# An attention and expert kernel on one core: where the sums of the input weights are made, and who adds the last key block

## The chip, the core and the metric

The kernel runs on one core of a Trainium2 chip. A core has four engines that compute, each with its own queue of instructions: TensorE (PE in the profile, PEld for its weight loads), VectorE (DVE), ScalarE (ACT) and GpSimd (POOL). SyncE (SP) only issues DMA transfers. The metric is the device time of one execution in microseconds (us); lower is better. The kernel before was run five times: median 883.84 us, from 883.41 to 883.97.

## The reference, cut to what matters

```python
# attention: 4 batches x 8 heads, 768 tokens, head size 64; 6 hash bits
q_bucket, k_bucket = hashes of q and k by the signs of q @ proj, k @ proj
mask = q_bucket[:, :, :, None] == k_bucket[:, :, None, :]
scores = np.where(mask, q @ k.T / np.sqrt(64), -1e9)
attn = np.exp(scores - scores.max(-1))
attn = attn / (attn.sum(-1) + 1e-09)
attn_out = attn @ v
# then x: 3072 tokens x 512, from all heads
h = x @ w_in            # 512 x 2048
r = np.maximum(h, 0.0)
out = (r * r) @ w_out   # 2048 x 512
```

The weights arrive as 64-bit floats; the kernel turns them into 32-bit ones itself.

## The kernel before

There are two stages. The first computes the attention, the second the two large products; this change touches only the first.

**The attention stage.** The loop `for pr in range(NP)` goes over sixteen pairs of heads. For each pair and each of six key blocks of 128 keys, `score` multiplies keys and queries on TensorE into PSUM (tiles `st`), and ScalarE takes the exponential into a tile `e`, a weight for each key and query. `attend` multiplies the values with these weights into `xo`. The softmax needs the sum over all keys as well: `add_up(pr, kt)` lets VectorE add block `kt` onto the tile `total` (128 partitions by 1536 numbers; key block 1 adds blocks 0 and 1). What is left, the sum over the 128 partitions, is made on TensorE in `sum_up` by a product with `ones` (four matmuls, one for each head and half of the queries, each to its own 32 columns of the array). VectorE turns the result over (`flip`), takes the reciprocal (`once`) and places it (`both`); TensorE spreads it over the partitions of each head (`spread`), and VectorE multiplies it into the output (`recs`, `x_t`, in `normalize`). A DMA on SP writes `x_t` to DRAM.

**Two ways to add block 5.** The dictionary `sums` names three pairs, 4, 5 and 8. In all other pairs VectorE adds blocks 1 to 5. In the three it adds only up to block 4, and `sum_up` gives TensorE a second source: the tile `e` of block 5 is multiplied with `ones` as well, four matmuls more, added up in the same PSUM tile.

**The weights beside it.** While the pairs run, the 32 pieces of both weight matrices are brought in and rounded, two pieces a pair: `load_weight` (a DMA on SP), `part_weight` on VectorE, `place_power` on ScalarE, `round_weight` on VectorE (L171, L176, L179). Pieces 0 to 15 are those of `w_in`; they stay in SBUF in two tiles, `ins[0]` (complete early in pair 4) and `ins[1]` (complete early in pair 8). The second stage multiplies by a scheme with seven products in place of eight, and for it needs sums and differences of the quarters of `w_in`. `sums_in(c)` makes four of them, `s1` to `s4`, for one of four groups of columns `c`: four VectorE instructions (L513 to L516) and, through `put_factor`, two DMAs on SP for each, which write the sum into `w_in_7` in DRAM. Before the change `sums_in(0)`, `(1)` and `(2)` stand at the end of pairs 4, 5 and 8, in the place of the add of block 5, and `sums_in(3)` at the start of pair 15.

**The order.** Each engine works through its instructions in the order in which the program issues them; this order is written out by hand. At the start of a pair VectorE has the transposes of q and k for the next pair (`features`), then `round_weight`, then `flip`, `once` and `both` for the pair before, then the add of blocks 0 and 1, then `recs` and `x_t`. TensorE has the scores of blocks 0 and 1, the hash of the next pair, `tot`, the last two `attend` of the pair before, and the spread. SP has the loads of q and k two pairs ahead, the write of a rounded piece, the load of a raw piece, then the write of `x_t`, the load of the values, and in the middle of the pair another piece. PSUM tiles of `st`, `hash` and `tot` share three buffers; `xo` has one.

The second stage loads its units of `w_in_7` from pair 13 on (`load_unit`); `load_x` and `sum_x` prepare its other operand.

Of the kernel before, what the change touches and what calls it, by code (L numbers as in the profile page):

```python
# [8 lines left out]
FP32 = mybir.dt.float32  # L9
# [6 lines left out]
ALU = mybir.AluOpType  # L16
# [18 lines left out]
def kernel(  # L35
# [10 lines left out]
    nc = tc.nc  # L46
# [6 lines left out]
    P = 128  # L53
    SB = S // P
    HS = S // 2
    NFT = DM // P
    NFF = DFF // P
    NP = B * H // 2
# [36 lines left out]
    p_t = first.enter_context(tc.tile_pool(name="p_t", bufs=1))  # L95
# [8 lines left out]
    def turn(name):  # L104

        return ps_s.tile([P, 2, 512], FP32, name=name, tag="turn")
# [4 lines left out]
    NIN = 2 * NFT  # L111
# [6 lines left out]
    def goal(i):  # L118
        if i < 2 * NIN:
            return ins[i // NIN][:, i % NIN // 2, i % 2]  # L120
        return p_t.tile([P, DM], FP32, name="out_piece", bufs=3)

    def load_weight(i):
        src, r, c = pieces[i]
        if src.dtype != U64:
            goals[i] = goal(i)
            nc.sync.dma_start(out=goals[i], in_=src[r:r + P, c:c + PIECE])
            return
        raw = p_w.tile([P, PIECE, 2], U32, name="raw", bufs=3)
        nc.sync.dma_start(  # L130
            out=raw.rearrange("p f w -> p (f w)"),
            in_=src.bitcast(U32)[r:r + P, 2 * c:2 * (c + PIECE)],
        )
        raws[i] = raw
# [64 lines left out]
    def put_factor(n, c, t):  # L199

        for f in range(NFT // 2):
            rs = t[:, f].rearrange("p (r c) -> p r c", c=P)
            nc.sync.dma_start(
                out=w_in_7[c // P:c // P + rs.shape[1], :, PLACE[n], f].rearrange("r p c -> p r c"), in_=rs
            )
# [16 lines left out]
    ones = const.tile([P, 32], FP32, name="ones")  # L222
# [156 lines left out]
    def weigh(pr):  # L379

        t = bits[pr, 1]
        nc.scalar.activation(out=t, in_=t, func=ACTF.Copy, scale=gains)

    weights = {}

    def score(pr, kt):

        e = ring[len(weights) % NRING]
        weights[pr, kt] = e
        key = slice(kt * P, (kt + 1) * P)  # L390
        sts = []

        def products(st, lo, hi, src, first):
            for h in range(2):
                rows = slice(h * D, (h + 1) * D)
                nc.tensor.matmul(  # L396
                    out=st[:, h, 0:hi - lo], lhsT=src[pr, 1][rows, key],
                    rhs=src[pr, 0][rows, lo:hi], start=first, stop=not first,
                )


        if (pr, kt) == (0, 0):
            for lo, hi in CUTS:
                sts.append(turn("st"))
                products(sts[-1], lo, hi, feat, True)
        for i, (lo, hi) in enumerate(CUTS):
            if len(sts) <= i:
                sts.append(turn("st"))
                products(sts[i], lo, hi, bits, True)
                products(sts[i], lo, hi, feat, False)  # L410
            else:
                products(sts[i], lo, hi, bits, False)
            nc.scalar.activation(  # L413
                out=e[:, :, lo:hi], in_=sts[i][:, :, 0:hi - lo], func=ACTF.Exp, scale=scale
            )

    totals, outs, recs = {}, {}, {}

    def add_up(pr, kt):

        if kt == 1:
            totals[pr] = p_n.tile([P, 2, S], FP32, name="total")
            nc.vector.scalar_tensor_tensor(
                out=totals[pr], in0=weights[pr, 0][:, :, 0:S], scalar=SB * TINY,
                in1=weights[pr, 1][:, :, 0:S], op0=ALU.add, op1=ALU.add,
            )
        else:
            nc.vector.tensor_tensor(  # L428
                out=totals[pr], in0=totals[pr], in1=weights[pr, kt][:, :, 0:S], op=ALU.add
            )  # L430
# [17 lines left out]
    def sum_up(pr, tot):  # L448


        tot = tot[:, 0]
        srcs = [totals[pr]] + [weights[pr, SB - 1]] * (pr in sums)
        for src in srcs:
            for c in range(2):
                for h in range(2):
                    g = 2 * h + c
                    nc.tensor.matmul(  # L457
                        out=tot[g * 32:(g + 1) * 32, 0:HS], lhsT=ones,
                        rhs=src[:, h, c * HS:(c + 1) * HS],
                        start=src is srcs[0], stop=src is srcs[-1],  # L460
                    )
        flip = p_n.tile([P, HS], FP32, name="flip")
        nc.vector.transpose(out=flip, in_=tot[:, 0:HS])
        once = p_n.tile([P, NB], FP32, name="once")
        nc.vector.reciprocal(
            out=once, in_=flip.rearrange("p (n f) -> p n f", f=32)[:, :, 0]
        )
        both = p_n.tile([P, 2, NB], FP32, name="both")
        nc.vector.tensor_tensor(
            out=both, in0=which,  # L470
            in1=once.rearrange("p (o n) -> p o n", o=1).to_broadcast([P, 2, NB]), op=ALU.mult,
        )
        onces[pr] = both
# [38 lines left out]
    def sums_a(a11, a12, a21, a22, s1, s2, s3, s4):  # L512
        nc.vector.tensor_tensor(out=s1, in0=a21, in1=a22, op=ALU.add)  # L513
        nc.vector.tensor_tensor(out=s3, in0=a11, in1=a21, op=ALU.subtract)
        nc.vector.tensor_tensor(out=s2, in0=s1, in1=a11, op=ALU.subtract)
        nc.vector.tensor_tensor(out=s4, in0=a12, in1=s2, op=ALU.subtract)  # L516

    def minus(out, in0, in1):
        nc.vector.tensor_tensor(out=out, in0=in0, in1=in1, op=ALU.subtract)  # L519

    NS = PIECE // 2

    def sums_in(c):

        j, h = divmod(c, 2)
        t, at = ins[j], slice(h * NS, (h + 1) * NS)
        nf = NFT // 2
        sums = [p_t.tile([P, nf, NS], FP32, name=f"s_in{n}", bufs=2) for n in range(4)]
        sums_a(
            t[:, 0:nf, 0, at], t[:, nf:NFT, 0, at], t[:, 0:nf, 1, at], t[:, nf:NFT, 1, at], *sums  # L530
        )
        for n in range(4):
            put_factor(3 + n, c * NS, sums[n])

    X_0 = 3 * PB
    sums = {NIN // 2: 0, NIN // 2 + 1: 1, NIN: 2}

    xs = {}

# [41 lines left out]
    with tc.manual_schedule():  # L584
# [21 lines left out]
        for pr in range(NP):  # L606
            a, b = 2 * pr, 2 * pr + 1
            more = pr + 1 < NP

            def prepare():  # L610

                hash_bits(pr + 1, turn("hash"))
                for w in (1, 0):
                    signs(pr + 1, w)


            if pr + 2 < NP:
                load_pair(pr + 2)
            if pr == X_0:
                load_x(0)  # L620
            if not more:
                sums_in(3)
            if more and pr > 0:
                for w in range(2):
                    features(pr + 1, w)
            if pr > 0:
                round_weight(b - 2)
                load_weight(b)
            score(pr, 0)
            if pr == 0:  # L630
                first_keys(1, turn("hash"))
            score(pr, 1)
            if pr > 0:
                finish(pr - 1, prepare if more else None)
            add_up(pr, 1)
            if pr == 0:
                for w in range(2):
                    features(1, w)
            if pr > 0:
                normalize(pr - 1)  # L640


            if pr == X_0 + 1:
                for n in range(2):
                    load_unit(n)
            part_weight(a)
            score(pr, 2)
            score(pr, 3)
            if pr == 0:
                prepare()  # L650
            elif more:
                weigh(pr + 1)
            place_power(a)
            attend(pr, 0)
            attend(pr, 1)
            for kt in (2, 3):
                add_up(pr, kt)
            if more:
                load_values(pr + 1)


            round_weight(a)
            part_weight(b)
            if more:
                load_weight(a + 2)
            score(pr, 4)
            score(pr, 5)
            if pr == 0:
                weigh(1)
            place_power(b)  # L670
            attend(pr, 2)
            attend(pr, 3)
            add_up(pr, 4)

            if pr not in sums:
                add_up(pr, 5)
            if pr in sums:
                sums_in(sums[pr])
        sum_x(0, 1)
        finish(NP - 1)  # L680
        normalize(NP - 1)
# [526 lines left out]
        for i in range(NCHUNK):  # L1208
            for s in range(NR):
# [8 lines left out]
                if i == 0 and r in THEN:  # L1218
                    m = THEN.index(r)
# [15 lines left out]
                for n in range(2):  # L1235
                    m = 2 * ((i - 1) * NR + s) + n
# [243 lines left out]
```

## Time and profile before

| | |
|---|---|
| median of five runs | 883.84 us |
| the profiled execution | 884.08 us |
| its span, from the first to the last instruction | 882.2 us |
| PE busy in the span | 867.8 us (98%) |
| PEld busy | 520.2 us (59%) |
| DVE busy | 755.7 us (86%) |
| ACT busy | 391.7 us (44%) |
| POOL busy | 106.9 us (12%) |
| granted TensorE clock | 0.997 of full speed |
| `total` adds on VectorE (L428) | 61 of 1756 ns |
| `tot` matmul records from `total` (L457) | 128, median 498 ns |
| `tot` matmul records from `e` (L457) | 24, median 486 ns |
| sums of the input weights (L513 to L516) | 16, of 682 to 692 ns |

A matmul of 32-bit floats appears as two records. Records of one engine overlap where an instruction starts before the one ahead of it is done, so the distance of two starts tells more than a duration. The attention stage ends at about 335 us of the span. The shares of busy time above are means over both stages.

### The profile page before, as it was taken

The numbers are of one execution on the slowest core, as the hardware profiler recorded it, in microseconds if no ns is written. First come the engines' busy times: TensorE is split into PE (matmuls) and PEld (weight loads), VectorE is DVE, ScalarE is ACT, GpSimd is POOL, SyncE is SP. The second block draws the span as 40 slices with busy tenths as digits, with TensorE's granted clock in tenths as the row PEclk, the third lists the DMA queues.
The fourth block names the chain that finished last, engine by engine and source line by source line (L and its number), as shares of the span: only waits on it lengthen the run. The fifth ranks groups of instructions, "written<-read, shape, count | busy, mean of one in ns | idle before, by whom it ended". The sixth has DMA issues, their size and how long they took to land.

```text
span 882.2 us, 12164 instructions
## 1 busy us (share of the span) xinstructions
PE 867.8 (98%) x4364; PEld 520.2 (59%) x4364; DVE 755.7 (86%) x1096; ACT 391.7 (44%) x673; POOL 106.9 (12%) x172
## 2 busy tenths in 40 slices
PE   8999999999999999999999999999999999999996
PEld 4444444444444444444688875556888755568885
DVE  5899999999999998888779978888889788888875
ACT  5988878888888861222211123332111233321110
POOL 2000000000000000564222021111100211110002
PEclk9999999999999999999999999999999999999998
DMA  9678779989778545989897775436847744455565
GB/s 164 141 152 136 198 179 188 184 278 212 147 167 188 158 149 187 307 259 290 281 353 245 185 164 170 158 116 227 295 143 183 176 156 157 130 166 149 161 174 104
DMA packets 224131, 167.09 MB, mean 189 GB/s; under 512 B 164448, under 2 KB 181344, under 8 KB 224064
## 3 DMA queue, kind: packets, MB, share of 16 engines
q1 hardware_dynamic: 189152, 87.19, 40.9%
q0 software_dynamic: 12528, 41.30, 15.0%
q10 hardware_dynamic: 22384, 37.76, 14.2%
q8 instruction: 36, 0.59, 0.3%
q14 instruction: 31, 0.25, 0.1%
HBM read 124.52 MB, written 41.68 MB: 188 GB/s over the span
## 4 chain that ended last, share of the span: by engine, by line
PE 94%; DVE 2%; ACT 1%; DMA 1%; issue 1%; ACTq 0%; DVEq 0%
PE acc L708 40%; PE st L396 17%; PE acc L927 16%; PE xo L438 13%; PE acc L880 5%; PE tot L457 2%; PE hash L346 1%; DVE total L428 1%; DMA k_nat<-in_k_dram 1%; ACT e L413 1%; ACT bits L356 1%; DMA w_in<-s_in 0%; DVE out_piece L179 0%; DVE power L171 0%; ACT small L160 0%
## 5 line engine op out<-in xcount | busy, mean ns | idle before, releaser
L413 ACT ACTIVATE e<-st 128x1024 f32<-128x1024 f32 x192 | 145.1, 810 | 46.9 <-PE st L396 42.7
L396 PE MATMUL st<-feat,feat 64*128 64x512 f32 (+1 forms) x768 | 150.4, 483 | 0.0
L438 PE MATMUL xo<-e,v_nat 128*64 128x512 f32 (+1 forms) x768 | 134.8, 492 | 0.0
L708 PE MATMUL acc<-b,leaf 128*128 128x256 f32 x600 | 133.4, 380 | 1.0 <-issue 1.0
L708 PEld LDWEIGHTS acc<-b,leaf 128*128 128x128 f32 x600 | 113.7, 190 | 17.8 <-issue 2.5
L428 DVE TENSOR_TENSOR total<-total,e 128x1536 f32<-128x1536 f32 x61 | 107.1, 1756 | 4.4
L438 PEld LDWEIGHTS xo<-e,v_nat 128*64 128x64 f32 x768 | 51.3, 136 | 82.4 <-issue 75.2
L927 PE MATMUL acc<-t_x,w_unit 128*128 128x512 f32 x192 | 90.2, 592 | 0.0
L396 PEld LDWEIGHTS st<-feat,feat 64*128 64x128 f32 x768 | 66.0, 188 | 33.7 <-issue 24.1
L708 PE MATMUL acc<-t,leaf 128*128 128x256 f32 x336 | 76.2, 380 | 0.0
L356 ACT ACTIVATE bits<-hash,lifts 32x384 bf16<-32x384 f32 x120 | 68.6, 572 | 3.2 <-issue 1.3
L708 PEld LDWEIGHTS acc<-t,leaf 128*128 128x128 f32 x336 | 63.7, 190 | 9.1 <-DVE t L519 0.5
L792 DVE SCALAR_TENSOR_TENSOR b<-h 128x512 f32<-128x512 f32 x96 | 65.7, 691 | 3.0
L396 PE MATMUL st<-bits,bits 64*128 64x256 bf16 (+1 forms) x384 | 63.0, 325 | 1.8 <-ACT e L413 1.4
L927 PE MATMUL acc<-x,w_unit 128*128 128x512 f32 x128 | 60.2, 592 | 0.0
L708 PE MATMUL acc<-x,w_unit 128*128 128x512 f32 x128 | 56.6, 594 | 0.0
L708 PE MATMUL acc<-b_t,leaf 128*128 128x256 f32 x240 | 53.8, 379 | 0.0
L927 PEld LDWEIGHTS acc<-t_x,w_unit 128*128 128x128 f32 x192 | 36.5, 190 | 28.9 <-issue 26.8
L715 ACT COPY two<-acc 128x256 f32<-128x256 f32 (+1 forms) x29 | 12.5, 431 | 87.7 <-PE acc L708 66.0
L715 ACT COPY one<-acc 128x256 f32<-128x256 f32 (+1 forms) x29 | 12.5, 431 | 86.1 <-PE acc L708 42.0
L708 PEld LDWEIGHTS acc<-b_t,leaf 128*128 128x128 f32 x240 | 45.5, 190 | 6.2
L396 PEld LDWEIGHTS <-bits 64*128 64x128 bf16 x384 | 23.3, 93 | 41.5 <-issue 37.9
(161 smaller groups left out, 1170.2 us busy)
## 6 DMA issues: line engine op xcount, KB each, us to landing
leaf<-w_out ACTq DMA_DIRECT2D x142, 256.0 KB, 3.1
w_unit<-w_in SPq DMA_DIRECT2D x16, 640.0 KB, 4.0
raw<-in_moe_w_in_dram SPq DMA_DIRECT2D x16, 512.0 KB, 5.9
raw<-in_moe_w_out_dram SPq DMA_DIRECT2D x16, 512.0 KB, 4.3
w_unit<-w_in SPq DMA_DIRECT2D x8, 896.0 KB, 7.9
w_out<-sums POOLq DMA_DIRECT2D x16, 448.0 KB, 6.8
sum<-w_in SPq DMA_DIRECT2D x16, 448.0 KB, 4.7
v_nat<-in_v_dram SPq DMA_DIRECT2D x16, 384.0 KB, 4.4
```

The source lines that it names most:

```text
L346: nc.tensor.matmul(out=banks[g * NR_B:(g + 1) * NR_B, h, 0:HS], lhsT=projs[rows], rhs=feat[pr, w][rows, c * HS:(c + 1) * HS], start=True, ...
L356: nc.scalar.activation(out=t[h * D:h * D + NR_B, c * HS:(c + 1) * HS], in_=hashed[pr, w][at, h, 0:HS], func=ACTF.Sign, scale=HUGE, bias=li ...
L396: nc.tensor.matmul(out=st[:, h, 0:hi - lo], lhsT=src[pr, 1][rows, key], rhs=src[pr, 0][rows, lo:hi], start=first, stop=not first,)
L413: nc.scalar.activation(out=e[:, :, lo:hi], in_=sts[i][:, :, 0:hi - lo], func=ACTF.Exp, scale=scale)
L428: nc.vector.tensor_tensor(out=totals[pr], in0=totals[pr], in1=weights[pr, kt][:, :, 0:S], op=ALU.add)
L438: nc.tensor.matmul(out=xo[h * D:(h + 1) * D, lo:hi], lhsT=nat[pr, "v_nat"][:, h, kt * D:(kt + 1) * D], rhs=weights[pr, kt][:, h, lo:hi], s ...
L457: nc.tensor.matmul(out=tot[g * 32:(g + 1) * 32, 0:HS], lhsT=ones, rhs=src[:, h, c * HS:(c + 1) * HS], start=src is srcs[0], stop=src is sr ...
L708: nc.tensor.matmul(out=acc[to], lhsT=a(i), rhs=b(i), start=first and i == 0, stop=last and i == n - 1, skip_group_check=True,)
L715: nc.scalar.copy(out=t, in_=acc[of])
L792: nc.vector.scalar_tensor_tensor(out=out, in0=h, scalar=0.0, in1=h, op0=ALU.max, op1=ALU.mult)
L880: nc.tensor.matmul(out=out, lhsT=w[:, a], rhs=b, start=start, stop=stop, skip_group_check=True)
L927: nc.tensor.matmul(out=acc[to], lhsT=w[:, PLACE[a], f], rhs=bt[b](f), start=first and f == 0, stop=last and f == NFT // 2 - 1, skip_group_ ...
```

## The change

The second source in `sum_up` is gone: TensorE makes the sum over the partitions from `total` alone, in every pair. In all pairs VectorE adds block 5 onto `total` at the end of the pair.

The sums of the input weights are cut into single steps. `sum_in(m)` makes sum `n` of column group `c`, with `c, n = divmod(m, 4)`: one VectorE instruction and its two DMAs. `sums` now says which steps each pair makes: one in each of the pairs 4 to 14, two in pair 9, and the last four in pair 15. They stand near the start of the pair, behind `round_weight` and `load_weight`, ahead of the scores. The four sums of pair 15 stood ahead of `round_weight` before, and stand behind it now.

```diff
@@ sum_up @@
-        srcs = [totals[pr]] + [weights[pr, SB - 1]] * (pr in sums)
-        for src in srcs:
-            for c in range(2):
-                for h in range(2):
-                    g = 2 * h + c
-                    nc.tensor.matmul(
-                        out=tot[g * 32:(g + 1) * 32, 0:HS], lhsT=ones,
-                        rhs=src[:, h, c * HS:(c + 1) * HS],
-                        start=src is srcs[0], stop=src is srcs[-1],
-                    )
+        for c in range(2):
+            for h in range(2):
+                g = 2 * h + c
+                nc.tensor.matmul(
+                    out=tot[g * 32:(g + 1) * 32, 0:HS], lhsT=ones,
+                    rhs=totals[pr][:, h, c * HS:(c + 1) * HS], start=True, stop=True,
+                )
@@ in place of sums_in @@
+    in_sums = {}
+
+    def sum_in(m):
+
+        c, n = divmod(m, 4)
         j, h = divmod(c, 2)
         t, at = ins[j], slice(h * NS, (h + 1) * NS)
         nf = NFT // 2
...
+        a11, a12, a21, a22 = (
+            t[:, f:f + nf, g, at] for g in range(2) for f in (0, nf)
+        )
+        s = in_sums[m] = p_t.tile([P, nf, NS], FP32, name=f"s_in{n}", bufs=2)
+        if n == 0:
+            nc.vector.tensor_tensor(out=s, in0=a21, in1=a22, op=ALU.add)
+        else:
+            minus(s, *(
+                (in_sums[4 * c], a11), (a11, a21), (a12, in_sums.get(4 * c + 1))
+            )[n - 1])
+        put_factor((3, 4, 5, 6)[n], c * NS, s)
...
-    sums = {NIN // 2: 0, NIN // 2 + 1: 1, NIN: 2}
+    todo = list(range(16))
+    sums = {}
+    for pr in range(NIN // 2, NP):
+        n = 16 if pr == NP - 1 else 1 + (pr == NIN + 1)
+        sums[pr], todo = todo[:n], todo[n:]
@@ in the loop over the pairs @@
-            if not more:
-                sums_in(3)
             if more and pr > 0:
                 for w in range(2):
                     features(pr + 1, w)
             if pr > 0:
                 round_weight(b - 2)
                 load_weight(b)
+                for m in sums.get(pr, ()):
+                    sum_in(m)
             score(pr, 0)
...
             add_up(pr, 4)
-
-            if pr not in sums:
-                add_up(pr, 5)
-            if pr in sums:
-                sums_in(sums[pr])
+            add_up(pr, 5)
```

More of the change, by code (lines that the diff above doesn't have):

```diff
@@ L521 @@
     NS = PIECE // 2
-    def sums_in(c):
+    in_sums = {}
+    def sum_in(m):
+        c, n = divmod(m, 4)
         j, h = divmod(c, 2)
@@ L527, in sums_in @@
         nf = NFT // 2
-        sums = [p_t.tile([P, nf, NS], FP32, name=f"s_in{n}", bufs=2) for n in range(4)]
-        sums_a(
-            t[:, 0:nf, 0, at], t[:, nf:NFT, 0, at], t[:, 0:nf, 1, at], t[:, nf:NFT, 1, at], *sums
-        )
-        for n in range(4):
-            put_factor(3 + n, c * NS, sums[n])
-    X_0 = 3 * PB
-    sums = {NIN // 2: 0, NIN // 2 + 1: 1, NIN: 2}
+        a11, a12, a21, a22 = (
+            t[:, f:f + nf, g, at] for g in range(2) for f in (0, nf)
+        )
+        s = in_sums[m] = p_t.tile([P, nf, NS], FP32, name=f"s_in{n}", bufs=2)
[6 more added lines that the diff above has]
+        put_factor((3, 4, 5, 6)[n], c * NS, s)
+    X_0 = 3 * PB
+    todo = list(range(16))
[3 more added lines that the diff above has]
+        sums[pr], todo = todo[:n], todo[n:]
     xs = {}
```

## The prediction

> **What bounds the kernel now.** I read the slices of the whole span first, then the attention stage pair by pair, then the order of the instructions inside a pair, and the chain of waits last.
>
> ```profile
> PE   8999999999999999999999999999999999999996
> DVE  5899999999999998888779978888889788888875
> ```
>
> One slice is 22 us. The change lies in the first 15 slices (the sixteen pairs). There TensorE and VectorE both read 9, so the slices don't say which one sets the pace. The stretches from one reciprocal sum to the next do. Columns: stretch, its length, busy us and number of instructions of PE, PEld, DVE, ACT and POOL, granted clock, DMA share, GB/s.
>
> ```profile
> 116.06:136.61 20.55, 20.55 (x158) 9.38 (x158) 19.29 (x25) 17.07 (x26) 0.00 (x0) 1.00 0.76 181
> 136.61:156.52 19.91, 19.91 (x150) 9.13 (x151) 18.55 (x22) 16.44 (x25) 0.00 (x0) 1.00 0.97 185
> 156.52:176.43 19.91, 19.91 (x150) 9.14 (x151) 18.55 (x23) 17.07 (x26) 0.00 (x0) 1.00 0.90 181
> ```
>
> Each ends where the sum of a pair is transposed, early in the next pair. The first closes pair 5, one of the three pairs in `sums`; the others close pairs 6 and 7. All ten stretches that I measured from 95.51 to 296.51 are 20.55 (pairs 4, 5, 8) or 19.90 to 19.91 (the rest). So such a pair costs 0.64 more. Two causes are possible: PE runs eight more matmul records, or VectorE does four factor sums in place of one add. The instructions on PE decide, the sum of pair 5 first and that of pair 6 below:
>
> ```profile
> 134.24 0.88 PE L346 MATMUL hash<-feat,projs 64*32 64x384 f32 x16
> 135.05 0.85 PE L457 MATMUL tot<-total,ones 128*32 128x384 f32 x8
> 135.72 0.83 PE L457 MATMUL tot<-e,ones 128*32 128x384 f32 x8
> 136.48 2.81 PE L438 MATMUL xo<-e,v_nat 128*64 128x512 f32 x16
> ...
> 154.80 0.88 PE L346 MATMUL hash<-feat,projs 64*32 64x384 f32 x16
> 155.60 0.85 PE L457 MATMUL tot<-total,ones 128*32 128x384 f32 x8
> 156.38 2.81 PE L438 MATMUL xo<-e,v_nat 128*64 128x512 f32 x16
> ```
>
> Read the starts, since the durations overlap. From the first `tot` to `xo` it is 1.43 for pair 5 and 0.78 for pair 6. The difference, 0.65, is the whole difference of the pairs. The four matmuls of a source (eight records) go to four column groups and overlap: 0.65 for all, though one takes 0.49.
>
> VectorE around the transpose `flip` of pair 6, which comes early in pair 7:
>
> ```profile
> 155.17 0.69 DVE L179 SCALAR_TENSOR_TENSOR in<-top,power 128x512 f32<-128x512 f32 x1
> 156.52 0.58 DVE L463 STREAM_TRANSPOSE flip<-tot 128x384 f32<-128x384 f32 x1 [0.66 <-PE tot L457]
> 157.14 0.23 DVE L465 RECIPROCAL once<-flip 128x12 f32<-128x12 f32 x1
> 157.40 0.18 DVE L469 TENSOR_TENSOR both<-which,once 128x24 f32<-128x24 f32 x1
> 157.50 1.75 DVE L423 SCALAR_TENSOR_TENSOR total<-e,e 128x1536 f32<-128x1536 f32 x1
> ```
>
> It stands idle for 0.66 until PE has done `tot`. Before the `flip` of pair 5 that idle time is 0.63, although VectorE had 0.77 more to do (four sums from 129.72 to 132.25, 2.53, against an add of 1.76). So VectorE follows PE here.
>
> **A rule against this reading.** The Trainium skill (Perfetto Trace Analysis, Identifying the Most-Contended Engine) holds that busy time of matmuls is no measure, that TensorE is to be judged by the share of its weight loads, VectorE by its occupancy, and that the engine with most is the one to optimize. By it TensorE has 9.13 of 19.91, 46%, and VectorE 18.55, 93%: VectorE would bind, and moving work onto it would cost (second rival). The rows say otherwise: the pair grew by PE's 0.65 while VectorE's idle time stayed. I go by the rows.
>
> **The change part by part.**
>
> *Removed on PE:* the `tot<-e` matmuls of pairs 4, 5 and 8, on the path, 3 x 0.64 to 0.65 = 1.93.
>
> *Added on VectorE:* the add of key block 5 in the same three pairs, 3 x 1.76 = 5.3. It stands where four sums of 0.68 stood (one every 0.6 to 0.7). One sum now comes back at the pair's start, 0.61, so these pairs have 2.53 - 1.76 - 0.61 = 0.16 less to do. The new wait is `tot` on that add. In pair 6 the add ends at 152.21 and `tot` starts at 155.60: 3.4 spare.
>
> *Moved on VectorE:* nine sums go into pairs that had none: 6, 7, 9 (two) and 10 to 14. Their row is
> ```profile
> L514 DVE TENSOR_TENSOR s_in<-in x4: 680/682/685, 109.8 to 312.6; 128x512 f32<-128x512 f32 x4
> ```
> The place is behind the last rounding step and ahead of `flip`, thus in the idle 0.66. A sum that starts 0.61 behind L179 (the step seen between the rounding instructions and between sums) runs from 155.78 to 156.46 and `flip` still starts at 156.52: cost 0. The skill (VectorE: DVE Perf Modes, The DRAIN you can't avoid) says that an operation starts only when the pipe of the one before is empty; then it ends at 155.86 + 0.68 = 156.54, and `flip` is 0.02 late, 0.2 over eleven pairs if nothing took it up. The starts in the trace, 0.6 apart for operations of 0.68, contradict the rule, and the next lines cover it anyway.
>
> *If the cover is gone:* behind `flip` stand `once` and `both` (done at 157.58); PE wants them for the spread at 159.02, 1.44 spare. `recs` starts at 159.32 behind PE's spread, 0.07 after L423's end; two more idle spots of 0.20 (before the adds at 162.16) and 0.12 (at 165.90, ScalarE's power) follow. In pair 14 `x_t` ends at 301.35 and PE writes the new `xo` at 302.54: 1.19 spare. So pair 9 with two sums has `flip` about 0.5 late, `recs` and `x_t` 0.45, the adds 0.25, the pair's end 0.1 to 0.2; pair 10 takes the rest up. PE sees none of it. In pairs 4 and 8 the sum reads the piece just rounded; dependent sums start 0.72 behind instead of 0.60: 0.1, taken up likewise.
>
> *DMAs:* each sum issues two of 128 KB on SP, 0.46 each (median). Behind them on SP are `x_t` and the values. In pair 13 SP is done at 278.11 and `x_t` comes at 281.47, so 3.3 us hold the one to two that are needed. The runs of eight at the ends of pairs 4, 5 and 8 (4.40 at 109.87) go away, and the next q and k loads start that much sooner. The later runs of loads wait for none of this: the first weight units are loaded in pair 13, their sums are written by pair 7. No row shows what these writes cost spread out: between -0.1 (no bunching) and +0.2 (late values); no VectorE wait in these pairs ends on a DMA, so I take 0.
>
> *Pair 15* is different: there VectorE is the path.
> ```profile
> 312.11 0.61 DVE s_in L513
> ...
> 329.75 1.77 DVE total L428
> 331.51 0.04 issue
> 331.56 0.85 PE tot L457 x8
> ```
> This is the chain of waits. VectorE works without a break from 312.03 to 331.50, and PE stands idle 1.03 for the last add. The change puts the rounding (1.94) ahead of the four sums (2.53) and lengthens neither: 0. Its eight DMAs end 1.94 later, at 318.9 instead of 316.96, before `x_t` at 321.19; the last raw piece is fetched some 3 us sooner. What VectorE is late by at the end of pair 14 would count in full, but there it waits for ScalarE at 305.89, and the sum's lateness is gone by then.
>
> *Sum:* -1.93. The profiled execution took 884.08, a span of 882.2 and 1.9 around it; it becomes 882.15. It stood 0.24 above the median of the runs, 883.84, so the forecast is **881.9**. Everything behind the stage shifts by the same.
>
> **The rivals.**
>
> 1. *Likeliest, 0.76:* as above, 881.9, give or take 0.3.
> 2. *VectorE sets the pair, 0.08, slower.* For it: 93% occupancy and the rule. Nine sums x 0.60 = 5.4, less 3 x 0.16, is +4.9, and PE's 1.93 isn't got: 888.7. It decides once the added sum exceeds the idle time of a pair, 0.66 + 0.20 + 0.12 = 0.98. Against it: one sum is 0.61.
> 3. *The last pair gives part back, 0.10.* If the sum of pair 14 isn't taken up, its 0.6 goes straight into the VectorE chain quoted last: -1.93 + 0.6 = -1.3, 882.5. For it: 20 us without a gap. Against: the gap at 305.89.
> 4. *PE gains more, 0.06.* The removed row's own busy time is 2.5 over three pairs: 881.3. Against it: neighbours overlap.
>
> That the matmuls stay is excluded: the second source is gone from the loop.
>
> **The numbers.** What a measurement of this kernel can tell from no change is about 0.2%, 1.77 us, and 1.93 lies just beyond it. Of the likeliest case 0.60 are counted faster and 0.16 within. Faster 0.60 + 0.06 = 0.66; within 0.16 + 0.10 = 0.26; slower 0.08. The range 881.2 to 882.9 takes in cases 1, 3 and 4.
>
> **What would show it.** Right: all pairs 19.91 from `flip` to `flip`; `tot` with 128 records; one sum ending within 0.1 of `flip`, whose idle time drops from 0.66 to about 0; PE's wait in pair 15 still 1.03. Wrong: stretches above 19.91, PE waiting for `both`, `xo` or a feature, or a longer wait for the last add.

## The result, and the profile after

| | before | changed |
|---|---|---|
| median, us | 883.87 (42 runs, 882.62 to 885.61) | 881.59 (22 runs, 880.84 to 882.53) |
| ratio to before | | 0.9974, 95% interval 0.9968 to 0.9980 |
| profiled execution: time, span | 884.08, 882.2 | 882.37, 880.6 |
| start of `tot` of the last pair | 331.56 | 329.67 |
| `total` adds on VectorE | 61 | 64 |
| `tot` records on PE | 152 | 128 |

The changed kernel is faster by 0.26%, some 2.3 us, with an interval of 1.8 to 2.8. The forecast was 1.93.

The stretches from `flip` to `flip`, with the columns of the prediction (length, busy time and number of instructions of PE, PEld, DVE, ACT, POOL, clock, DMA share, GB/s). These two close pairs 4 and 5:

```profile
95.57:115.48 19.91, 19.91 (x150) 9.14 (x150) 19.16 (x25) 17.07 (x26) 0.00 (x0) 1.00 0.97 223
115.48:135.38 19.90, 19.90 (x150) 9.14 (x150) 19.16 (x23) 17.07 (x26) 0.00 (x0) 1.00 0.64 146
```

They were 20.55 and are like the others now. Only at pair 9, which has two sums, do the lengths from `flip` to `flip` differ (20.37, then 19.66 and 19.69), because that `flip` is late; PE's `tot` comes every 19.91 there too. VectorE's busy time, 19.29 here before, is 19.16; in the pairs without sums it rose from 18.55 to 19.15 (pair 6), and they did not get longer. The end of pair 5 on PE, in order of time:

```profile
133.66 0.88 PE L346 MATMUL hash<-feat,projs 64*32 64x384 f32 x16
134.46 0.85 PE L455 MATMUL tot<-total,ones 128*32 128x384 f32 x8
135.24 2.81 PE L438 MATMUL xo<-e,v_nat 128*64 128x512 f32 x16
```

From `tot` to `xo` there are 0.78 us where there were 1.43. VectorE at the same place:

```profile
134.04 0.69 DVE L179 SCALAR_TENSOR_TENSOR in<-top,power 128x512 f32<-128x512 f32 x1
134.65 0.69 DVE L516 TENSOR_TENSOR s_in<-in 128x512 f32<-128x512 f32 x1
135.38 0.58 DVE L460 STREAM_TRANSPOSE flip<-tot 128x384 f32<-128x384 f32 x1
136.00 0.23 DVE L462 RECIPROCAL once<-flip 128x12 f32<-128x12 f32 x1
```

The sum starts 0.61 behind the last rounding step and ends at 135.34, and `flip` starts 0.92 behind `tot`, exactly as it did before (155.60 to 156.52): the sum lies in the idle time and delays nothing. The chain of waits in the last pair:

```profile
312.17 0.61 DVE s_in L533
...
312.80 1.89 DVE s_in L516 x3
...
327.86 1.77 DVE total L428
329.63 0.04 issue
329.67 0.85 PE tot L455 x8
```

VectorE is still the path there, and PE still waits 1.03 for the last add. The whole stretch has moved forward by 1.89.

The span fell by 1.6, somewhat less. The largest difference behind the stage is one place where PE idles for a time that differs from profile to profile, here 0.58 more (order of time on PE, the kernel before and then the changed one):

```profile
455.37 1.97 PE L708 MATMUL acc<-b,leaf 128*128 128x256 f32 x8 [0.96 <-issue]
```

```profile
453.89 1.97 PE L712 MATMUL acc<-b,leaf 128*128 128x256 f32 x8 [1.54 <-issue]
```

In the ten profiles of this study, one of each kernel, this idle time lies between 0.48 and 1.59. No run shows what it depends on.

### The profile page after: what moved, and what is told of

The parts are those of the page before. It is cut to its first block, busy times and chain, and to the rows that moved or that the text cites. A ratio compares the mean times of both kernels' runs of the same rounds, so it can differ in the third digit from the quotient of the medians.

```text
span 880.6 us, 12132 instructions
## 1 busy us (share of the span) xinstructions
PE 866.0 (98%) x4340; PEld 519.7 (59%) x4340; DVE 760.5 (86%) x1099; ACT 391.9 (45%) x673; POOL 106.9 (12%) x172
## 4 chain that ended last, share of the span: by engine, by line
PE 95%; DVE 2%; ACT 1%; issue 1%; DVEq 0%
PE acc L712 40%; PE st L396 17%; PE acc L931 16%; PE xo L438 13%; PE acc L884 5%; PE hash L346 1%; PE tot L455 1%; DVE total L428 1%; ACT e L413 1%; ACT bits L356 1%; PE xo L326 1%; PE tp L309 0%; DVE s_in L516 0%; DVE out_piece L179 0%; DVE power L171 0%
## 5 line engine op out<-in xcount | busy, mean ns | idle before, releaser
L428 DVE TENSOR_TENSOR total<-total,e 128x1536 f32<-128x1536 f32 x64 | 112.4, 1756 | 5.2 <-ACT small L160 0.5
L719 ACT COPY two<-acc 128x256 f32<-128x256 f32 (+1 forms) x29 | 12.5, 432 | 87.7 <-PE acc L712 69.1
L719 ACT COPY one<-acc 128x256 f32<-128x256 f32 (+1 forms) x29 | 12.5, 432 | 86.5 <-PE acc L712 48.3
```

The lines of the kernel that those rows point to most:

```text
L428: nc.vector.tensor_tensor(out=totals[pr], in0=totals[pr], in1=weights[pr, kt][:, :, 0:S], op=ALU.add)
L719: nc.scalar.copy(out=t, in_=acc[of])
```

## The experiments

All times are medians in us; the ratio is to the kernel before, with its 95% interval. The kernel before had a median of 884.07 beside the first four runs and of 883.71 beside the last four. The theory: TensorE sets the pace of all pairs but the last, so the gain is the twelve matmuls (24 records) that went; VectorE's share is covered as long as it fits into idle time at its place. Rivals: VectorE sets the pace; or the gain came from spreading the sums and their DMAs.

**The two parts alone.** First the spreading without the removal:

```diff
+    SECOND = 4, 5, 8
...
+        srcs = [totals[pr]] + [weights[pr, SB - 1]] * (pr in SECOND)
+        for src in srcs:
...
-            add_up(pr, 5)
+            if pr not in SECOND:
+                add_up(pr, 5)
```

> The changed kernel, but in pairs 4, 5 and 8 TensorE again takes block 5 as a second source and VectorE leaves that add out; the sums of the input weights stay spread. Theory (TensorE's matmuls were the gain): nothing gained, 883.9, ratio to before 1.000, pairs 4, 5 and 8 at 20.55, the others at 19.91. Rival (the gain came from spreading the sums and their DMAs): the gain stays, about 881.6, ratio 0.997, with the three pairs below 20.55.

Measured: 883.77, ratio 0.9993 (0.9985 to 1.0002). Pairs 4, 5 and 8 take 20.55, 20.56 and 20.55 from `flip` to `flip`, the others from pair 2 to pair 13 19.90 to 19.91. VectorE in order of time, the `flip` of pair 4:

```profile
115.67 0.58 DVE L463 STREAM_TRANSPOSE flip<-tot 128x384 f32<-128x384 f32 x1 [2.56 <-PE tot L457]
```

It waits 2.56 for PE in such a pair, having neither the add of block 5 nor the run of four sums to do, and the pair is no shorter for it. So the spreading brings nothing that the times can show, and VectorE isn't what makes these pairs long.

Then the removal without the spreading, made from the kernel before:

```diff
-        srcs = [totals[pr]] + [weights[pr, SB - 1]] * (pr in sums)
+        srcs = [totals[pr]] + []
...
-            if pr not in sums:
-                add_up(pr, 5)
+            add_up(pr, 5)
             if pr in sums:
                 sums_in(sums[pr])
```

> The kernel before with the second source taken out and block 5 added by VectorE in all pairs, the sums left in runs of four at the ends of pairs 4, 5 and 8. Theory: TensorE saves 1.93, but VectorE has 2.53 more than a plain pair in each of the three, against some 1.0 of idle time and 1.44 of slack ahead of the spread; TensorE waits about 0.5 in pairs 4 and 8 and more in pair 5, which follows at once, about 2.9 in all: 884.8 (884 to 885.5), slower than the changed kernel by some 3. Rival (VectorE sets every pair): before plus three adds, 889.2. Rival (VectorE is covered whatever it does): 881.9.

Measured: 886.76, ratio 1.0027 (1.0017 to 1.0038): slower, in kind as the theory said, but 2 us more than it said. Pairs 4, 5 and 8 take 21.70, 21.63 and 21.71. PE in order of time, early in pair 5, right behind the four sums of pair 4, and VectorE there:

```profile
114.34 1.62 PE L346 MATMUL hash<-feat,projs 64*32 64x384 f32 x16 [0.92 <-DVE feat L333]
```

```profile
114.12 0.93 DVE L333 STREAM_TRANSPOSE feat<-k_nat 128x768 f32<-128x768 f32 x1
```

PE waits not for the spread, as I had expected, but earlier, for the hash of the next pair. Its operands are the two transposes, of q and of k. The hash of q starts at 114.34, behind the first; that of k needs the second, which ends at 115.05, so the row lasts 1.62 instead of 0.88. In the kernel before, early in pair 7, VectorE had done the second transpose in time:

```profile
153.03 0.94 DVE L333 STREAM_TRANSPOSE feat<-k_nat 128x768 f32<-128x768 f32 x1
```

It ended at 153.97 and the hash started at 154.80, 0.83 to spare. In pairs 4, 5 and 8 of that kernel the four sums stood in place of the add and made the transposes only 2.53 - 1.76 = 0.77 late, just within it. With the add beside them it is 2.53, 1.7 too many, and the pairs grew by 1.7 to 1.8. I had looked only at what stands behind the place of the new sums, and these old sums stand ahead of the transposes.

**The price of the second source in all pairs.** As in the first experiment, with

```diff
-    SECOND = 4, 5, 8
+    SECOND = range(NP)
```

> The changed kernel with the second source in all sixteen pairs and no add of block 5 on VectorE at all. Theory (TensorE sets pairs 0 to 14, VectorE the last one): 15 x 0.64 more, and in the last pair 0.65 more less the 1.03 that TensorE now waits there: +9.2, 890.8, ratio to before 1.0078. Rival (VectorE sets the pair): 1.76 less work on VectorE in every pair, so faster than the changed kernel, below 880.

Measured: 890.63, ratio 1.0068 (1.0054 to 1.0082); forecast 890.8. A stretch of it:

```profile
118.22:138.77 20.55, 20.55 (x158) 9.39 (x158) 17.39 (x23) 17.08 (x26) 0.00 (x0) 1.00 0.67 141
```

VectorE has 1.76 less to do in every pair (17.39 of 20.55), and every pair is longer by 0.64. A kernel that VectorE paced would have become faster. This settles the first rival for the pairs before the last.

**How much VectorE can take.** Each of the first twelve sums is made twice, and in a further run three times (`1 + 2 * (m < 12)`); the repeats write the same numbers and issue no DMA:

```diff
-        if n == 0:
-            nc.vector.tensor_tensor(out=s, in0=a21, in1=a22, op=ALU.add)
-        else:
-            minus(s, *(
-                (in_sums[4 * c], a11), (a11, a21), (a12, in_sums.get(4 * c + 1))
-            )[n - 1])
+        for _ in range(1 + 1 * (m < 12)):
+            if n == 0:
+                nc.vector.tensor_tensor(out=s, in0=a21, in1=a22, op=ALU.add)
+            else:
+                minus(s, *(
+                    (in_sums[4 * c], a11), (a11, a21), (a12, in_sums.get(4 * c + 1))
+                )[n - 1])
         put_factor((3, 4, 5, 6)[n], c * NS, s)
```

> The changed kernel with the first twelve sums each made twice on VectorE (the same instruction again, DMAs once). Theory: a pair has about 0.98 idle on VectorE and one sum takes 0.61 of it, so the second one is 0.23 too many in ten pairs and 1.45 in pair 9; slack ahead of the spread hides the start of it, and what is late at the end of pair 14 counts in the last pair: +3.7 at most, 883.5 to 885.3. Rival (VectorE sets every pair): 12 x 0.61, 888.9. Rival (more cover than counted): 881.6, no change.

Measured: 882.89, ratio 0.9986 (0.9979 to 0.9993), less than the 883.5 at which my range began. The stretch of pair 6, and VectorE in order of time at its end:

```profile
135.80:155.71 19.91, 19.91 (x150) 9.15 (x148) 19.49 (x26) 17.08 (x26) 0.00 (x0) 1.00 0.78 147
```

```profile
153.77 0.69 DVE L179 SCALAR_TENSOR_TENSOR in<-top,power 128x512 f32<-128x512 f32 x1
154.38 1.41 DVE L516 TENSOR_TENSOR s_in<-in,s_in 128x512 f32<-128x512 f32 x2
155.71 0.58 DVE L460 STREAM_TRANSPOSE flip<-tot 128x384 f32<-128x384 f32 x1
```

With 0.61 + 0.72 = 1.33 us of sums the pair is still 19.91, and no idle time is listed on VectorE's rows between one `flip` and the next. So a pair had 1.33 to give, not the 0.98 of the prediction. Up to pair 8 the `flip` comes 1.64 behind `tot` instead of 0.92, 0.72 late, and PE doesn't mind: that is the slack ahead of the spread. In pair 9, with four sums, the slack isn't enough. What PE waited for in the stage (total, times, longest):

```profile
PE tot L455 <- DVE total L428: 1.4, 1, 1.4
PE xo L477 <- DVE both L466: 0.5, 1, 0.5
```

The wait of 0.5 is that of pair 9. From there to pair 13 `flip` stays 2.20 behind `tot`, since no pair has time left to catch up, and in the last pair PE's wait grew from 1.03 to 1.45. The two waits together make 0.9 of the 1.3 us by which this run is slower than the changed kernel.

> The changed kernel with the first twelve sums each made three times on VectorE (one more repeat than in the run before). Theory after that run (two sums leave VectorE without a gap and just at TensorE's 19.91): the third one, 0.72 in ten pairs and twice that in pair 9, is paid in full, so 8.6 over the run with two, near 891.5, and pairs of about 20.6. Rival (still covered): 883.

Measured: 892.72, ratio 1.0101 (1.0085 to 1.0117), 1.2 above the forecast; where that comes from is open. A stretch, and what PE waited for in the stage (total, times, longest):

```profile
137.63:158.26 20.63, 20.17 (x150) 9.03 (x148) 20.18 (x26) 17.07 (x26) 0.00 (x0) 1.00 0.74 142
```

```profile
PE xo L477 <- DVE both L466: 6.2, 9, 2.5
```

Beyond 1.33 each pair grows by the whole 0.72 of the third sum, and PE now waits for `both` at the spread. That is the point from which VectorE does set the pair.

**Place or number.** Runs of four again in pairs 4, 5 and 8, but behind the rounding step:

```diff
-        n = 16 if pr == NP - 1 else 1 + (pr == NIN + 1)
+        n = 4 * (pr in (4, 5, 8, NP - 1))
```

> The changed kernel with the sums in runs of four again, in pairs 4, 5 and 8, but behind the rounding step as in the changed kernel and not at the end of the pair. Theory (it is the place that counts: behind the transposes of q and k, ahead of the transposed sum, 1.44 spare): three times some 0.6, more in pair 5, which follows at once: near 884, and TensorE waits for the spread and not for the hash. Rival (only the number in a row counts, not the place): as with runs of four at the pairs' ends, 886.8. Rival (place alone is enough): 881.6.

Measured: 883.78, ratio 0.9999 (0.9991 to 1.0008), 2.2 above the changed kernel. PE's waits:

```profile
PE xo L477 <- DVE both L466: 1.6, 3, 0.9
```

None for the hash is left. The same removal with the same runs of four costs 886.76 ahead of the transposes and 883.78 behind them, so for runs of four the place makes 2.5 us by the ratios and 3 by the medians. Spreading them at the new place makes the other 2.2. Single sums at the old place were not run. By the rows one sum of 0.61 would fit into the 0.83 to spare there, and two in one pair, as in pair 9, would not; that is an estimate, so it isn't shown that the place matters once the sums are spread.

**The last pair.** Two sums in every second pair, so that pair 15 has none:

```diff
+        n = 1 + (pr < NP - 1 and pr % 2)
```

> The changed kernel with two sums in each of the pairs 5, 7, 9, 11 and 13, so that pair 15 has none. Theory (in the last pair VectorE is the path and its four sums, 2.53, make TensorE wait 1.03 for the last add): the wait goes, 1.03 less than the changed kernel, 880.5, ratio to before 0.9962; pairs stay at 19.91. Rival (the wait in the last pair has another cause, or the doubles come back as waits): 881.6 or more.

Measured: 881.29, ratio 0.9971 (0.9961 to 0.9982); the forecast was 880.5. In the trace PE's wait fell, but only by 0.6:

```profile
328.61 0.85 PE L455 MATMUL tot<-total,ones 128*32 128x384 f32 x8 [0.43 <-DVE total L428]
```

VectorE now starts its `recs` on time, at 316.06 behind the spread, but from there to the end of the last add it has 12.5 us of its own without a gap, and PE, done at 328.18, has 0.4 less. The pairs with two sums have `flip` 0.46 late and the next one back in time.

The second source in pair 15 alone, again as in the first experiment, with

```diff
-    SECOND = 4, 5, 8
+    SECOND = (NP - 1,)
```

> The changed kernel with the second source on TensorE in pair 15 alone, where VectorE then leaves out the add of block 5. Theory: VectorE has 1.76 less on the path, so TensorE's wait of 1.03 goes and its second source costs 0.65: 0.4 less, 881.2. Rival (the second source costs 0.65 anywhere and the wait has another cause): 882.2.

Measured: 881.27, ratio 0.9972 (0.9962 to 0.9982). PE in order of time:

```profile
328.28 0.85 PE L457 MATMUL tot<-total,ones 128*32 128x384 f32 x8
328.95 0.83 PE L457 MATMUL tot<-e,ones 128*32 128x384 f32 x8
```

It waits no more: the second source costs 0.67 and removes 1.03. In the traces both versions end the first stage earlier than the changed kernel (spans of 879.7 against 880.6); their medians are 0.3 below it, which the intervals don't tell from nothing. Neither is shown to be better.

## Why the prediction was right

*What bounds the pairs.* Right: TensorE. The prediction took this from two starts in the trace and from VectorE's idle time, against a rule that points at the engine with the highest occupancy. (Beside the weight loads the rule names a second measure of TensorE, its share of peak arithmetic, which was not worked out.) Taking 1.76 off VectorE in each pair and giving PE 0.65 made every pair 0.64 longer.

*The removal, 3 x 0.64 to 0.65.* Right: the three pairs went from 20.55 to 19.91, and the last `tot` starts 1.89 earlier. The median moved by 2.3, and 1.93 lies in its interval of 1.8 to 2.8; whether the rest is more than noise can't be told.

*The adds in pairs 4, 5 and 8, and the sum in the idle 0.66.* Right, down to the end of the sum at 135.34 ahead of `flip` at 135.38. In pair 9, with two sums, `flip` was expected 0.5 late; it is 0.46 late (195.57 instead of 195.11), pair 10's about 0.2, and pair 11's is in time. The Trainium skill's rule that VectorE starts an operation only when the pipe is empty (VectorE: DVE Perf Modes, The DRAIN you can't avoid) doesn't describe these rows: starts lie 0.61 behind an operation of 0.69. The prediction left out that the same section lets a next operation start earlier where it isn't held.

*The idle time of a pair, 0.98.* Mis-sized: 1.33. Of its three terms 0.66 and 0.12 are idle times, counted from the end of one row to the start of the next, and a fourth spot, ahead of `recs`, was left out of the sum. Rows overlap by some 0.08 when nothing holds them up, so each idle spot hides that much more. Compare the starts around the `flip` of pair 6 in the kernel before with those in the run with each sum made twice, where nothing holds VectorE up: L179 to `flip` 1.35 against 0.61 from L179 to what stands behind it there, 0.74; L423 to `recs` 1.82 against 1.67, 0.15; L147 to the next add 0.55 against 0.34, 0.21; the two adds 3.74 against 3.53, 0.21; in all 1.31. It didn't matter for one sum of 0.61. It would have for a change that puts two into each pair.

*The DMAs, -0.1 to +0.2, taken as 0.* In the run that spreads them and keeps the matmuls the ratio is 0.9993 (0.9985 to 1.0002): nothing can be told.

*Pair 15.* Right: the four sums and the rounding changed places and PE's wait stayed 1.03. That VectorE is the path there was argued from the chain; the two last runs show it.

*The rivals.* VectorE as the bound is refuted below 1.33 us a pair and shown above it. The last pair gave nothing back. That PE gains the removed row's own busy time, 2.5 over three pairs, is refuted by the stretches, which became 0.64 shorter each and not 0.83; the median alone, 881.59, lies between 881.3 and 881.9 and couldn't have told. What the prediction did not see is that the old place of the sums had a nearer deadline, 0.83, than the new one, 1.44: with the sums left there in runs of four, the removal made the kernel 0.27% slower.

## What to carry to other kernels

When two engines are both busy over nine tenths, compare two periods of a loop that differ by known work: the engine whose extra work equals the extra time sets the pace. When work is put onto the other engine, find for the place where it goes the first thing behind it that the pacing engine waits for; two places on one queue can have deadlines 0.6 us apart, and for runs of four sums that decided here between 0.27% slower and no change. Measure slack from start to start, against the same sequence where nothing holds the engine up, and not by adding idle times.

## What the runs showed of the hardware

VectorE operations on 128x512 numbers of 32 bits, 0.68 to 0.69 us long, started 0.60 to 0.61 apart where they were independent and 0.72 apart where one read what the one before wrote, or wrote the same tile. Four matmuls of 32-bit floats with 384 columns, each to its own 32 columns of the array, took 0.64 to 0.67 us of TensorE's time together, in every pair where they were put (3, 16 or 1), though one record lasts 0.49.
